# Attention scores of a head pair: one PSUM allocation of two banks in place of two allocations of one bank

## The chip, the cores and the metric

The kernel runs on one core of one Trainium2 chip. The metric is device time in microseconds (us) of one execution. The engines are PE (matrix products, with PEld for its weight loads), DVE (vector), ACT (scalar), POOL (GpSimd) and SP, which issues the DMAs.

## The reference

The reference chains one attention block and two feed-forward blocks over 4 batches of 576 positions, 8 heads of 64.

```python
scores = (1/8) * q @ k.T                       # per batch and head, 576 x 576, causal mask
a = exp(scores - max); a /= a.sum() + 1e-9
local = a @ v
qp = phi(q)                                    # elu + 1
mem_out = (qp @ M_prev) / (qp @ z_prev + 1e-6)
x = g * mem_out + (1 - g) * local              # g = sigmoid(beta), per head; heads side by side: 512 columns
x = ((x @ w1) * (x @ w2)) @ w3 @ w_out         # 512 -> 1024 -> 1024 -> 512
out = (sigmoid(x @ w_gate) * (x @ w_val)) @ w_o # 512 -> 1536 -> 512
```

## The kernel before

The 8 heads are taken as 4 pairs `p`; one head of a pair lies on partitions 0 to 63, the other on 64 to 127. The 576 rows of queries are padded to 580 and cut into 5 row blocks `i` of 116. Row block `i` has 116*(i+1) columns of scores. For `i = 4` these are 580, more than a PSUM bank holds, so they are made in two halves of 290 columns (`n` = 0, 1).

One step of attention runs as follows. `s_part` (L552) makes the scores of both heads (`hh` = 0, 1) in PSUM. One DVE instruction for each head (L557) adds the mask, writes the result to SBUF (`p`) and takes the row extremum into `sm`; this text calls it the mask. ACT takes the exponential (`e_part`, L105). `n_part` (L580, L581, L583) makes the reciprocal on DVE and normalises both heads on POOL or DVE; in the startup always on POOL. PE transposes the result (`t_part`, L613) and multiplies it with `v` into `o` (`a_part`, L666 to L681), to which the memory part (`qt`, `mphi`) is added.

Names in the rows: `s0_1_4_1_0` is the score of batch 0, pair 1, row block 4, half 1, head 0. `t0_1_3` are transposes of row block 3 of pair 1. The last number of a name is a running number.

Weights arrive as 64-bit floats. They are converted in steps: ACT makes `cy` and `cr` (L199, L202), DVE shifts and masks bits (L210, L211), POOL adds (L215), then a split into a high and a low half on ACT and on DVE or POOL (L311, L313) gives tiles `wslot` and `wo`. In the startup PE multiplies `w3` with `w_out` once: eight blocks `wps0_0` to `wps0_7` of twelve products (L302), each with the weights `wo0` to `wo3`, and then eight more (`wps1_`) with `wo4` to `wo7`, two of them ahead of the first feed-forward product and the rest between such products. The buffers of `wo4` to `wo7` are those of `wo0` to `wo3`, and so are free only when `wps0_7` has been made.

The order of work: in the startup, which holds attention of batch 0 and the blocks `wps0_0` to `wps0_7`, a scheduler that keeps a timeline of its own at build time sets the order on each engine. From there on the order on PE is the program's: attention of batch `b + 1` is laid in small steps between the feed-forward products of batch `b` (`drive`), and the scheduler orders the other engines.

PSUM has 8 banks. The pools take 3 (`ps_f`, for feed-forward sums and some transposes), 2 (`ps_s`, scores), 1 (`ps_t`, transposes) and 2 (`ps_o`). A tile's buffer is given again when all that read the tile are done.

Of the kernel before, what the change touches and what calls it, by code (L numbers as in the profile page):

```python
# [7 lines left out]
F32 = mybir.dt.float32  # L8
# [9 lines left out]
T = 116  # L18
# [32 lines left out]
def tile_attention_memory_ffn(  # L51
# [20 lines left out]
    fp = ctx.enter_context(tc.tile_pool(name="fp", bufs=2))  # L72
    ap = ctx.enter_context(tc.tile_pool(name="ap", bufs=2))
    ps_f = ctx.enter_context(tc.tile_pool(name="ps_f", bufs=3, space=bass.MemoryType.PSUM))
    ps_s = ctx.enter_context(tc.tile_pool(name="ps_s", bufs=2, space=bass.MemoryType.PSUM))
    ps_t = ctx.enter_context(tc.tile_pool(name="ps_t", bufs=1, space=bass.MemoryType.PSUM))
    ps_o = ctx.enter_context(tc.tile_pool(name="ps_o", bufs=1, space=bass.MemoryType.PSUM))
    dr = ctx.enter_context(tc.tile_pool(name="dr", bufs=1, space=bass.MemoryType.DRAM))
# [370 lines left out]
    def attention(b, lag):  # L449
# [79 lines left out]
        def s_part(p, i, n):  # L529
            w = T * (i + 1)  # L530
            if n == 0:
                ps_ = []
                for hh in range(2):
                    name = f"p{b}_{p}_{i}_{hh}"
                    if first and np_["n"] % 2 == 0:
                        m = np_["n"] // 2 % P0
                        ps_.append(fp.tile([T, 2 * S], F32, tag=f"h{m}", name=name, bufs=1)[:, :SP])
                    else:
                        ps_.append(ap.tile([T, SP], F32, tag="p", name=name, bufs=PB))
                    np_["n"] += 1  # L540
                sp[p, i] = (ps_, ap.tile([T, 8], F32, tag="sm", name=f"sm{b}_{p}_{i}", bufs=6))
            ps_, sm = sp[p, i]
            c0, c1 = (0, w) if w <= 512 else ((0, SP // 2), (SP // 2, SP))[n]
            os_ = []
            for hh in range(2):
                ps = ps_s.tile([128, 512], F32, tag="s", name=f"s{b}_{p}_{i}_{n}_{hh}")
                os_.append(ps[:T, : c1 - c0])
            terms = [(qks[p], qks[p])] if first else [(parts[p][x], parts[p][y]) for x, y in ((0, 0), (1, 0), (0, 1))]
            for x, (q_, k_) in enumerate(terms):
                for hh in range(2):  # L550
                    r = slice(64 * hh, 64 * hh + 64)
                    nc.tensor.matmul(  # L552
                        os_[hh], q_[r, 0, i * T : (i + 1) * T], k_[r, 1, c0:c1],
                        start=x == 0, stop=x == len(terms) - 1,
                    )
            for hh in range(2):
                nc.vector.tensor_tensor_reduce(  # L557
                    out=ps_[hh][:, c0:c1],
                    in0=os_[hh],
                    in1=msk[:, SP - w + c0 : SP - w + c1],  # L560
                    scale=-0.125,
                    scalar=3.0e38 if n == 0 else sm[:, 2 * hh : 2 * hh + 1],
                    op0=ALU.add,
                    op1=ALU.min,
                    accum_out=sm[:, 2 * hh + n : 2 * hh + n + 1],
                )
# [140 lines left out]
        for k in range(NPAIR * NT + lag):  # L707
# [3 lines left out]
            if k < NPAIR * NT:  # L711
                p, i = divmod(k, NT)
                wgt = 0.25 + 0.25 * (i + 1)
                s_part(p, i, 0)
                yield wgt
                if i == NT - 1:
                    s_part(p, i, 1)
                    yield 0.0
                if i == 0:
                    mem = mem_steps(p)  # L720
                next(mem, None)
                e_part(p, i, 0)
                yield wgt + between(kk % NT)
                e_part(p, i, 1)
                yield wgt + between(kk % NT)
                n_part(p, i)
                if i > 0:
                    next(mem, None)
                if i == 3:
                    qt_part(p)  # L730
                if i == 0:
                    load_qk(p + 2 if first else p + 1)
                if i == 4:
                    split_qk(p + 1)
                if i == 4:
                    load_rest(p + 1)
                yield wgt + between(kk % NT)
                yield wgt + between(kk % NT)
                yield wgt + between(kk % NT)
            while ts:  # L740
                yield ts.pop(0)()
            if kk >= 0 and kk % NT == NT - 1:
                p = kk // NT
# [143 lines left out]
```

## Time and profile before

| | |
|---|---|
| median of 3 runs | 1093.98 us (1088.79 to 1095.29) |
| profiled execution | 1093.54 us |
| its span, first to last instruction | 1091.6 us |
| PE busy | 1059.9 us, 97% |
| DVE, ACT, POOL busy | 506.6, 486.9, 319.7 us |

The profiled execution is 0.44 us below the median. 1.94 us of it lie outside the span. PE's busy time counts every stretch in which a product is under way; products overlap, so the same busy time can hold more or fewer of them.

### The profile page before, as it was taken

Reading aid. Unit: us, or ns where it says so; the run is one execution under the profiler, and the core shown is the slowest. Engines: PE = TensorE matmul, PEld = TensorE weight load, DVE = VectorE, ACT = ScalarE, POOL = GpSimd, SP = SyncE. Lnnn points to the kernel's source line nnn. Section 1 sums busy time; section 2 is a strip of 40 time slices with the busy share of each in tenths; the row PEclk is TensorE's granted clock in tenths of the full one; section 3 lists DMA queues with packets and bytes.
Section 4 is the critical chain, followed back from the end, with each engine's and each line's share of the span. In section 5 each row is a group of like instructions: output and inputs, shape, how many; then the busy total and the mean of one; then the engine's idle time right before and its main releaser. Section 6 shows DMA issues by size and latency. Waiting matters only on the chain.

```text
span 1091.6 us, 19687 instructions
## 1 busy us (share of the span) xinstructions
PE 1059.9 (97%) x7616; PEld 947.9 (87%) x7616; DVE 506.6 (46%) x1215; ACT 486.9 (45%) x1066; POOL 319.7 (29%) x260
## 2 busy tenths in 40 slices
PE   6999899999999899999999999999999999999998
PEld 3555677898998799889999899889999899999998
DVE  7996898758666605554222506453223402212210
ACT  6787676666766625444222415444223312222210
POOL 5887676446655602222000303231000200000000
PEclk9999899999999899999999999999999999999999
DMA  8565688856888564444445365433455355554451
GB/s 274 164 228 174 227 252 273 301 180 232 302 280 297 193 215 157 164 148 151 160 155 174 123 199 160 136 129 117 157 174 169 99 155 179 169 169 164 158 178 56
DMA packets 69237, 201.75 MB, mean 185 GB/s; under 512 B 9624, under 2 KB 15896, under 8 KB 69144
## 3 DMA queue, kind: packets, MB, share of 16 engines
q1 hardware_dynamic: 69144, 200.50, 56.0%
q8 instruction: 60, 0.98, 0.4%
q14 instruction: 33, 0.27, 0.1%
HBM read 160.10 MB, written 40.37 MB: 184 GB/s over the span
## 4 chain that ended last, share of the span: by engine, by line
PE 65%; DVE 1%; DMA 1%; ACT 1%; issue 0%; POOL 0%; ACTq 0%; POOLq 0%
PE gv L302 21%; PE ab L302 15%; PE ot L302 13%; PE xw L302 7%; PE s L552 3%; PE t L613 2%; PE o L681 2%; PE o L666 1%; DMA k<-wslot 1%; PE o L674 1%; DMA r<-in_o_dram 0%; PE qt L650 0%; DVE wraw L210 0%; DVE wslot L313 0%; DVE p L557 0%
## 5 line engine op out<-in xcount | busy, mean ns | idle before, releaser
L302 PE MATMUL gv<-x,wslot 128*128 128x288 f32 x2304 | 308.6, 295 | 4.5 <-ACT gsb L105 3.0
L302 PEld LDWEIGHTS gv<-x,wslot 128*128 128x128 f32 x2304 | 305.9, 188 | 6.8 <-ACT gsb L105 3.7
L302 PE MATMUL ab<-x,wslot 128*128 128x288 f32 x1536 | 227.8, 300 | 0.0
L302 PEld LDWEIGHTS ab<-x,wslot 128*128 128x128 f32 x1536 | 207.0, 188 | 11.2 <-issue 8.2
L302 PE MATMUL ot<-hg,wslot 128*128 128x288 f32 x1152 | 166.2, 301 | 3.7 <-DVE hg L313 3.6
L302 PEld LDWEIGHTS ot<-hg,wslot 128*128 128x128 f32 x1152 | 156.5, 190 | 10.1 <-issue 4.6
L583 POOL TENSOR_SCALAR p<-p,sm,omg 116x116 f32<-116x116 f32 (+4 forms) x100 | 97.7, 980 | 213.0 <-DVE sm L581 137.3
L215 POOL TENSOR_TENSOR wraw<-wraw,cr 128x512 int32<-128x512 int32 x76 | 109.9, 1458 | 66.5 <-DVE wraw L211 60.6
L105 ACT ACTIVATE p<-p,sm 116x116 f32<-116x116 f32 (+4 forms) x160 | 93.0, 582 | 63.7 <-DVE sm L557 55.9
L557 DVE CUSTOM_DVE_ANT_0 p<-s,msk 116x116 f32<-116x116 f32 (+4 forms) x160 | 68.5, 454 | 109.7 <-PE s L552 109.4
L417 DVE TENSOR_TENSOR hgraw<-gv,gsb 128x288 f32<-128x288 f32 x96 | 43.8, 457 | 157.4 <-PE gv L302 134.5
L302 PE MATMUL xw<-h,wslot 128*128 128x288 f32 x768 | 111.4, 299 | 0.0
L302 PEld LDWEIGHTS xw<-h,wslot 128*128 128x128 f32 x768 | 103.1, 188 | 3.6 <-issue 2.5
L105 ACT ACTIVATE gsb<-gv 128x288 f32<-128x288 f32 x96 | 39.4, 411 | 108.6 <-PE gv L302 108.6
L495 POOL TENSOR_TENSOR me<-mphi,z 116x640 f32<-116x640 f32 x16 | 25.4, 1586 | 175.2 <-issue 174.4
L613 PE MATMUL t<-idf,p 116*116 116x116 f32 x480 | 69.7, 274 | 3.7 <-POOL p L583 2.6
L199 ACT ACTIVATE cy<-r 128x512 f32<-128x512 f32 x76 | 50.6, 675 | 50.6 <-issue 27.9
L613 PEld LDWEIGHTS t<-idf,p 116*116 116x116 f32 x480 | 54.6, 140 | 18.8 <-POOL p L583 7.9
L211 DVE SCALAR_TENSOR_TENSOR wraw<-cy,wraw 128x512 int32<-128x512 int32 x76 | 66.6, 898 | 0.2
L373 DVE TENSOR_TENSOR hraw<-ab,asb 128x288 f32<-128x288 f32 x64 | 29.2, 456 | 67.7 <-PE ab L302 65.0
L313 POOL TENSOR_TENSOR wslot<-wraw,wslot 128x512 fp32r<-128x512 f32 x36 | 47.9, 1330 | 35.2 <-ACT wslot L311 35.0
L311 ACT CAST hg<-hgraw 128x576 fp32r<-128x576 f32 x48 | 32.4, 674 | 57.8 <-DVE hgraw L417 57.8
(78 smaller groups left out, 1129.4 us busy)
## 6 DMA issues: line engine op xcount, KB each, us to landing
wslot<-k SPq DMA_DIRECT2D x180, 512.0 KB, 3.5
k<-wslot SPq DMA_DIRECT2D x60, 512.0 KB, 5.2
r<-in_gv_dram SPq DMA_DIRECT2D x24, 512.0 KB, 5.3
qk<-in_qk_dram SPq DMA_DIRECT2D x32, 290.0 KB, 3.8
r<-in_w3t_dram SPq DMA_DIRECT2D x16, 512.0 KB, 4.0
r<-in_w_dram SPq DMA_DIRECT2D x16, 512.0 KB, 5.1
r<-in_o_dram SPq DMA_DIRECT2D x12, 512.0 KB, 5.6
qnr<-in_qn_dram SPq DMA_DIRECT2D x16, 320.0 KB, 3.2
```

Source lines behind the costliest of these rows:

```text
L105: ins = nc.scalar.activation(**kw)
L199: nc.scalar.mul(y, hi, 2.0**-112)
L211: nc.vector.scalar_tensor_tensor(z, y, -(2**31), z, ALU.bitwise_and, ALU.bitwise_or)
L215: nc.gpsimd.tensor_tensor(z, z, tmp["r"], ALU.add)
L302: nc.tensor.matmul(ps, w[:, wi, blk, :], x[:, xi, cols : cols + n], start=first and part == 0, stop=last and part == 2,)
L311: nc.scalar.copy(dst[:, 0], src)
L313: eng.tensor_sub(dst[:, 1], src, dst[:, 0].bitcast(F32))
L417: nc.vector.tensor_mul(hraw[:, c0 : c0 + HS], pss[1][:, :HS], asb)
L552: nc.tensor.matmul(os_[hh], q_[r, 0, i * T : (i + 1) * T], k_[r, 1, c0:c1], start=x == 0, stop=x == len(terms) - 1,)
L557: nc.vector.tensor_tensor_reduce(out=ps_[hh][:, c0:c1], in0=os_[hh], in1=msk[:, SP - w + c0 : SP - w + c1], scale=-0.125, scalar=3.0e38 if ...
L583: lower(SHARE_N).tensor_scalar(ps_[hh][:, :w], ps_[hh][:, :w], sm[:, 6 + hh : 7 + hh], omg[:T, 2 * p + hh : 2 * p + hh + 1], ALU.mult, ALU ...
L613: nc.tensor.transpose(tp[:T, c : c + T], src[hh][:, j * T : (j + 1) * T], idf[:T, :T])
```

## The change

The pool of the scores has one buffer of two banks. `s_part` allocates one tile for both heads, and head `hh` takes bank `hh` of it. The products, the masks and the PSUM taken are the same as before.

```diff
-    ps_s = ctx.enter_context(tc.tile_pool(name="ps_s", bufs=2, space=bass.MemoryType.PSUM))
+    ps_s = ctx.enter_context(tc.tile_pool(name="ps_s", bufs=1, space=bass.MemoryType.PSUM))
...
-            os_ = []
-            for hh in range(2):
-                ps = ps_s.tile([128, 512], F32, tag="s", name=f"s{b}_{p}_{i}_{n}_{hh}")
-                os_.append(ps[:T, : c1 - c0])
+            ps = ps_s.tile([128, 2, 512], F32, tag="s", name=f"s{b}_{p}_{i}_{n}")
+            os_ = [ps[:T, hh, : c1 - c0] for hh in range(2)]
```

In the built program the first score product of a tile now waits for both masks of the tile before it; it used to be one wait for each head, on that head's own mask. The mask of head 0 now waits for the products of both heads. A name such as `s0_1_4_1` now stands for both heads, and line numbers behind the change are smaller by 2.

The order on PE differs in the first 316 of its 7,280 products, up to the block `wps0_5`, and is the same from there. The orders on the other engines differ most in the same stretch.

On DVE, in the startup, between the masks of the two halves of row block 4 of pair 0. Before:

```order
L210 TENSOR_SCALAR wraw1_337<-cy2_319 128x512
L211 SCALAR_TENSOR_TENSOR wraw1_337<-cy2_319,wraw1_337 128x512
L557 ISA p0_0_4_0_293,sm0_0_4_295<-s0_0_4_1_0_305,msk_82,sm0_0_4_295 116x290
L557 ISA sm0_0_4_295 116x1
L210 TENSOR_SCALAR wraw1_337<-cy3_406 128x512
L313 TENSOR_TENSOR wo1_302<-wraw0_219,wo1_302 128x512
L557 ISA p0_0_4_1_294,sm0_0_4_295<-s0_0_4_1_1_306,msk_82,sm0_0_4_295 116x290
```

Now (the masks of the first half stand just ahead of this piece):

```order
L210 TENSOR_SCALAR wraw2_479<-cy4_473 128x512
L313 TENSOR_TENSOR wo2_374<-wraw1_331,wo2_374 128x512
L211 SCALAR_TENSOR_TENSOR wraw2_479<-cy4_473,wraw2_479 128x512
L210 TENSOR_SCALAR wraw2_479<-cy5_486 128x512
L313 TENSOR_TENSOR wo3_450<-wraw1_331,wo3_450 128x512
L211 SCALAR_TENSOR_TENSOR wraw2_479<-cy5_486,wraw2_479 128x512
L210 TENSOR_SCALAR wraw3_572<-cy6_551 128x512
L211 SCALAR_TENSOR_TENSOR wraw3_572<-cy6_551,wraw3_572 128x512
L210 TENSOR_SCALAR wraw3_572<-cy7_641 128x512
L211 SCALAR_TENSOR_TENSOR wraw3_572<-cy7_641,wraw3_572 128x512
L313 TENSOR_TENSOR wslot1_524<-wraw2_479,wslot1_524 128x512
L555 ISA p0_0_4_0_289,sm0_0_4_291<-s0_0_4_1_300,msk_82,sm0_0_4_291 116x290
```

The conversions of `cy4` to `cy7` moved ahead of the second half's masks. Counted up to the reciprocal of that row block (L581 on `sm0_0_4`), 14 more DVE instructions stand ahead than before: 5 of L210, 5 of L211, 4 of L313.

On PE, in the startup, around the block `wps0_1`. Before, from the second half of row block 4 of pair 1:

```order
L552 MATMUL s0_1_4_1_0_546<-qk0_1_172 116x290
L613 MATMUL t0_1_2_0_1_606<-idf_80,p0_1_2_1_413 116x116 x3
L552 MATMUL s0_1_4_1_1_547<-qk0_1_172 116x290
L302 MATMUL wps0_1_619<-wo0_247,wslot1_534 128x512 x3
L302 MATMUL wps0_1_619<-wo1_302,wslot1_534 128x512 x3
L302 MATMUL wps0_1_619<-wo2_382,wslot1_534 128x512 x3
L302 MATMUL wps0_1_619<-wo3_460,wslot1_534 128x512 x3
L552 MATMUL s0_2_0_0_0_590<-qk0_2_207 116x116
L552 MATMUL s0_2_0_0_1_591<-qk0_2_207 116x116
L613 MATMUL t0_1_3_0_0_639<-idf_80,p0_1_3_0_451 116x116 x4
```

Now, from the last products of the block:

```order
L302 MATMUL wps0_1_606<-wo3_450,wslot1_524 128x512 x3
L550 MATMUL s0_1_4_0_530<-qk0_1_172 116x290 x2
L672 MATMUL o0_1_726<-pq0_1_185,vs0_1_327 64x232 x2
L611 MATMUL t0_1_3_0_0_625<-idf_80,p0_1_3_0_442 116x116 x4
L611 MATMUL t0_1_3_0_1_631<-idf_80,p0_1_3_1_443 116x116 x4
L550 MATMUL s0_1_4_1_535<-qk0_1_172 116x290 x2
L550 MATMUL s0_2_0_0_578<-qk0_2_206 116x116 x2
L550 MATMUL s0_2_1_0_617<-qk0_2_206 116x232 x2
L611 MATMUL t0_1_4_0_0_665<-idf_80,p0_1_4_0_527 116x116
L611 MATMUL t0_1_4_1_681<-idf_80,p0_1_4_0_527 116x116
```

Both halves of row block 4 moved from ahead of `wps0_1` to behind it, and the heads stand side by side. Around `wps0_3` it is the same for the second half of pair 2.

On POOL, at the end of the startup, around the split of `wo7`. Before:

```order
L215 TENSOR_TENSOR wraw10_1439<-wraw10_1439,cr20_1416 128x512
L215 TENSOR_TENSOR wraw10_1439<-wraw10_1439,cr21_1467 128x512
L215 TENSOR_TENSOR wraw11_1535<-wraw11_1535,cr22_1524 128x512
L313 TENSOR_TENSOR wo7_1271<-wraw7_1205,wo7_1271 128x512
L215 TENSOR_TENSOR wraw11_1535<-wraw11_1535,cr23_1557 128x512
```

Now:

```order
L215 TENSOR_TENSOR wraw10_1412<-wraw10_1412,cr20_1389 128x512
L215 TENSOR_TENSOR wraw10_1412<-wraw10_1412,cr21_1440 128x512
L313 TENSOR_TENSOR wo7_1246<-wraw7_1181,wo7_1246 128x512
L215 TENSOR_TENSOR wraw11_1507<-wraw11_1507,cr22_1496 128x512
L215 TENSOR_TENSOR wraw11_1507<-wraw11_1507,cr23_1529 128x512
```

The split of `wo7` moved ahead of one conversion. On ACT the cast of `wo7` has one `cy` and one `cr` fewer ahead of it.

## Rows read from the trace of the kernel before

**Rows 1.** Stretches: length; busy us of PE, PEld, DVE, ACT, POOL; granted clock; DMA share, GB/s.

```profile
0.00:46.60 46.60, 36.53 (x99) 18.18 (x99) 37.28 (x95) 33.84 (x79) 32.03 (x31) 1.00 0.71 228
46.60:56.17 9.57, 9.30 (x51) 4.63 (x49) 9.08 (x18) 7.29 (x16) 8.39 (x8) 1.00 0.57 172
56.17:106.43 50.26, 47.72 (x266) 27.89 (x265) 41.70 (x109) 40.29 (x99) 41.04 (x39) 1.00 0.62 198
106.43:131.90 25.47, 22.24 (x104) 16.36 (x103) 22.10 (x40) 16.81 (x36) 16.85 (x13) 0.87 0.69 225
131.90:1091.60 959.70, 944.15 (x7103) 880.85 (x7102) 396.43 (x956) 388.64 (x838) 221.43 (x172) 1.00 0.55 181
```

**Rows 2.** The same view, score products alone (L552).

```profile
56.17:106.43 50.26, 14.95 (x55) 5.62 (x54) 1.00 0.62 198
```

**Rows 3.** Timeline of PE in the startup: start, us, count, [idle before].

```profile
41.89 4.71 PE L302 MATMUL wps<-wo,wslot 128*128 128x512 f32 x11
...
56.17 3.06 PE L302 MATMUL wps<-wo,wslot 128*128 128x512 f32 x12
59.16 0.46 PE L552 MATMUL s<-qk 64*116 64x116 f32 x4
...
62.29 0.65 PE L552 MATMUL s<-qk 64*116 64x232 f32 x4
...
65.40 0.85 PE L552 MATMUL s<-qk 64*116 64x348 f32 x4
...
67.41 1.03 PE L552 MATMUL s<-qk 64*116 64x464 f32 x2 [0.72 <-DVE sm L557]
...
76.68 0.75 PE L552 MATMUL s<-qk 64*116 64x290 f32 x4
...
78.70 0.74 PE L552 MATMUL s<-qk 64*116 64x290 f32 x2
...
127.16 4.96 PE L302 MATMUL wps<-wo,wslot 128*128 128x512 f32 x12
```

**Rows 4.** Groups on DVE in the first 46 us: busy us, mean ns.

```profile
L211 DVE SCALAR_TENSOR_TENSOR wraw<-cy,wraw 128x512 int32<-128x512 int32 x9 | 9.5, 1051 | 0.1
...
L210 DVE TENSOR_SCALAR wraw<-cy 128x512 int32<-128x512 int32 x9 | 5.4, 599 | 0.1
L313 DVE TENSOR_TENSOR wo<-wraw,wo 128x512 fp32r<-128x512 f32 x4 | 4.8, 1191 | 0.0
```

**Rows 5.** Timeline: DVE's first instruction; reciprocal and normalising of row block 4, pair 0.

```profile
5.48 0.17 DVE L777 TENSOR_SCALAR g<-g 128x8 f32<-128x8 f32 x1 [5.48 <-ACT g L776]
...
28.24 0.15 DVE L581 RECIPROCAL sm<-sm 116x2 f32<-116x2 f32 x1
...
28.57 2.84 POOL L583 TENSOR_SCALAR p<-p,sm,omg 116x580 f32<-116x580 f32 x2 [1.07 <-DVE sm L581]
```

**Rows 6.** Timeline: row block 4 of pair 1, from mask to transposes.

```profile
57.36 0.51 DVE L557 CUSTOM_DVE_ANT_0 p<-s,msk,sm 116x290 f32<-116x290 f32 x1
...
58.25 0.77 ACT L105 ACTIVATE p<-p,sm 116x580 f32<-116x580 f32 x1
...
62.38 2.62 POOL L583 TENSOR_SCALAR p<-p,sm,omg 116x580 f32<-116x580 f32 x2 [0.40 <-DVE sm L581]
...
63.30 0.71 PE L613 MATMUL t<-idf,p 116*116 116x116 f32 x5 [0.35 <-POOL p L583]
...
65.06 0.41 PE L613 MATMUL t<-idf,p 116*116 116x116 f32 x2 [1.04 <-POOL p L583]
```

**Rows 7.** Line L552 from 105 to 900 us: PE's idle time before it, by releaser.

```profile
  DVE sm L557: 4.9, 9
```

**Rows 8.** Timeline: the split of wo7 and the products behind it.

```profile
123.94 0.73 PE L302 MATMUL wps<-wo,wslot 128*128 128x512 f32 x2 [1.60 <-ACT wo L311]
...
124.51 1.73 POOL L313 TENSOR_TENSOR wo<-wraw,wo 128x512 fp32r<-128x512 f32 x1
...
126.30 0.80 PE L302 MATMUL wps<-wo,wslot 128*128 128x512 f32 x1 [1.62 <-POOL wo L313]
```

## The prediction

> **What bounds the kernel now.** I read the busy times by stretch first [rows 1]. From 131.90 us to the end PE has a product under way in 944.15 of 959.70 us, and the order on PE there is the same after the change. The startup, 0 to 131.90 us, is where orders move, so it is cut at places that both kernels have: the end of the weight block wps0_0 (46.60 us), the starts of wps0_1 (56.17) and wps0_5 (106.43), and the first feed-forward product (131.90). In the first stretch PE is busy 36.53 of 46.60 us, in the next two 9.30 of 9.57 and 47.72 of 50.26, and in the last 22.24 of 25.47. DVE is nearly as full: 37.28, 9.08, 41.70 and 22.10 us. So the startup has no single bound: PE, DVE and POOL are linked by the chain score, mask, exponential, reciprocal, normalising, transposes, and the weight conversion lies between on DVE, ACT and POOL.
>
> Next come the costs on PE. Two heads on the two halves of the partitions run side by side: four 290-column products of two heads take 0.75 us, two products of one head alone 0.74 us [rows 3]. A second head that stands alone costs as much as the pair. In the startup many heads stand alone before; now none does.
>
> PE's speed is the third thing to see. Eleven weight products take 4.71 us at 41.89, twelve take 3.06 us at 56.17 and 4.96 us at 127.16 [rows 3]. In the stretch from 106.43 the mean granted clock is 0.87, elsewhere 1.00 [rows 1]; the view also prints 1.00 for the first stretch, though the products there, 0.43 us each, are as slow as at the lower of the two levels (1.2 and 2.4 GHz), and those at 56.17 take 0.255.
>
> **The change part by part.** Products, masks and PSUM stay; waits and order change. I take the stretches in turn, against the profiled execution of 1093.54 us, whose span is 1091.6 (0.44 us under the median; I count it as equal).
>
> *To the end of wps0_0.* The transposes of row block 4 of pair 0 must come before wps0_0, and they need its reciprocal and normalising. The reciprocal ran at 28.24 us, and the normalising of both heads took 2.84 us [rows 5]. Now 14 more DVE instructions stand ahead of it: 5 x 0.599 + 5 x 1.051 + 4 x 1.191 = 13.0 us [rows 4] (for the two splits into wslot I take the time of those into wo). That would put it at 41.2 us, less what DVE's idle time takes up: DVE is idle 46.60 - 37.28 = 9.3 us here [rows 1], of which 5.48 lie ahead of its first instruction [rows 5], so at most 3.8 us. So it comes at 37.4 to 41.2, the normalising is done at 40.2 to 44.1, then the last five transposes take 0.71 [rows 6] to twice that at the lower speed, and the block 12 x 4.71 / 11 = 5.1 us: its end comes at 46.0 to 50.6 us, which is -0.6 to +4.0 against 46.60. I take +2, near the middle. What covered this before was slack: the normalising was done at 31.4 us, and eleven of the block's products only began at 41.89 [rows 3, 5].
>
> *wps0_0 to wps0_1.* The four lone scores of row block 4 of pair 1 leave this stretch (4 x 0.74), the 348-column pair of row block 2 enters (0.85 [rows 3]). That is -2.1 us, and the idle 0.27 us [rows 1] may go too. The first part of o0_1 moves in from the next stretch; it nets out over the two. Against it stands a wait for row block 2's normalising, which was well ahead before. I take -1, from -2.3 to +2.
>
> *wps0_1 to wps0_5.* Scores fill 14.95 us of PE here [rows 2]. In the new order the stretch holds the pairs of both halves for pair 1 (2 x 0.75) and two full sets, 0.46 + 0.65 + 0.85 + 1.03 + 2 x 0.75 = 4.49 each [rows 3] (for 464 columns a lone head's time, taken as the pair's). So 10.48 us, or -4.5. PE's idle time here is 50.26 - 47.72 = 2.5 us, which the new order may remove. The cost: the second half of row block 4 stood ahead of wps0_1 and wps0_3, whose 3 us hid the chain to its transposes. Now it stands behind them, with only the pairs 0.46, 0.65 and 0.85 and five transposes (0.71) between, 2.7 us of work. The chain as such is two masks of 0.51, two exponentials of 0.77, 0.3 for the reciprocal and 2.62 for the normalising [rows 6], 5.5 us; so PE waits 2.8 us each time. By what it took before, with the conversion between, it is longer: the mask ended at 57.87, the last transposes started at 65.06 [rows 6], 7.2 us, 8.2 with the masks, and the wait would be 5.5. Two pairs: 5.6 to 11 us. Where head 1's exponential runs beside head 0's normalising, it might be 4. Other row blocks wait for a mask more, 0 to 2 us. Sum: from -4.5 - 2.5 + 4 = -3 to -7 + 11 + 2 = +6. I take +1, nearer to the row than to the bare chain, because POOL and DVE stay over 80% busy here.
>
> *wps0_5 to the first feed-forward product.* The first score of batch 1 moves in here (+0.4), and the transposes of pair 3 follow their scores closely (0 to +2, taken +0.5). PE waited 1.60 and 1.62 us for wo7 [rows 8]. Its split on POOL started at 124.51, though the cast that it needs was done by 123.94; the conversion ahead of it is now behind. With one cy and one cr fewer ahead of the cast on ACT, I take -1.1 (0 to -2). The block behind it ran at the lower clock, 4.96 where 3.06 is the other level; whether the shorter wait keeps the clock is open: half of 1.9, -1. Sum -1.2, from -3.5 to +2.5.
>
> *After 131.90.* The order on PE is the same. In batches 1 to 3 the heads already alternate, and head 1's wait comes one product behind head 0's, so waiting for both masks at once moves only head 0's first product. From 105 to 900 us PE and PEld idle 4.9 us before scores because of masks, in 9 places [rows 7]. Twelve fifth row blocks could wait one mask longer, but head 1 waited for that mask anyway. +0.5, from -2 to +2. Fewer semaphore waits and signals: no row shows their price; they can give back some of those 4.9 us at most, and I take 0.
>
> Sum: +2 - 1 + 1 - 1.2 + 0.5 = +1.3. 1093.54 + 1.3 is 1094.9; I say **1095 us**.
>
> **The rivals.** *Startup stalls in full, slower.* Both exposures at their long end and wps0_0 late: +4 + 2 + 6 + 2 = +14, 1107 us. For it: POOL and DVE queues are full, and PE cannot pass a waiting transpose. Against: conversion has been done earlier by then, so the queues are freer. It decides over 1% when the two exposures come to about 7 us each (-7 + 14 + 1 there, +4 and -1 ahead of it). Chance 0.10.
>
> *PE drops to its lower level in the waits.* At 124 us PE worked 0.73 us between waits of 1.60 and 1.62, and the products after that were slow [rows 3, 8]; the new waits at pairs 1 and 2 look alike. Five blocks at 4.96 in place of 3.06 cost 9.5 us: with the +1.3, 1104 us, and a few us more with slow scores. Against: waits of 1.04 us in the same stretch left the clock at 1.00 [rows 1, 6]. Chance 0.05. The Trainium skill speaks for this one ("TensorE: Matmul & The Clock Gate", section on a second failure mode, PSUM-queue depth-cycling): when a kernel cycles PSUM buffers so that PE pauses often between groups of products, the clock swings between its levels. This trace shows one such swing in the startup, at 0.87.
>
> *The work freed on PE is kept, faster.* If the chain to the transposes hides whole behind other work, the stretches give -0.6, -2.3, -4.5 - 2.5 and -3.5, together -13.4: 1080 us. For it: 6.6 us of scores on PE are gone for certain, and the conversion is further on. Against: 2.7 us of work would have to hide a chain of 5.5. It decides over 1% when both exposures together stay under 2.5 us. Chance 0.09.
>
> *It does nothing.* The moved orders cancel and the pairing saves time that PE would have waited anyway: 1093.5 us. PE's later stretch sets the time, and it is equal. Chance 0.16; it cannot be told from my forecast by time, only by the stretches.
>
> **How the numbers follow.** The forecast has 0.60. A measurement here tells about 1%, 11 us, from no change. Faster by more than that: the third rival, 0.09. Slower: the first two, 0.15. Within: 0.76. The range of 8 in 10 goes over the forecast and no effect, with the unknown terms combined (about -6 and +7 around 1095) and the spread of the runs, some 3 us: 1086 to 1105 us.
>
> **What would show it.** wps0_0 ends at 47 to 50 us; all scores of the startup show as pairs (x4 in a row for each tile); lone-score time on PE in the startup falls by 6 us or more; PE waits on POOL ahead of transposes grow from 1.4 us to over 5 in the two places behind wps0_1 and wps0_3; the wait at wo7 falls under 3 us; wps0_5 starts within 5 us of 106.43; the stretch from the first feed-forward product to the end keeps its 959.7 us within 2. I am wrong if that last stretch changes by more, if the order at 46 us costs over 5 us, or if the clock falls inside 46 to 106 us.

## The result, and the profile after

The changed kernel takes 1110.31 us (median, 1109.67 to 1110.45) where the kernel before takes 1093.9 in the same comparison: a ratio of 1.0147, interval 1.0127 to 1.0167. It is slower by 16 us, outside the range of the prediction. The profiled execution took 1110.45 us, with a span of 1108.6.

First come the busy times of the changed kernel by stretch, cut at the same places as [rows 1]: the end of `wps0_0`, the starts of `wps0_1` and `wps0_5`, the first feed-forward product.

```profile
0.00:50.20 50.20, 25.21 (x93) 13.72 (x93) 41.98 (x88) 35.17 (x80) 35.48 (x31) 0.80 0.73 239
50.20:65.29 15.09, 10.38 (x59) 5.66 (x58) 13.73 (x28) 10.21 (x23) 14.67 (x14) 0.82 0.58 181
65.29:122.54 57.25, 48.63 (x261) 29.36 (x259) 31.62 (x102) 34.40 (x87) 30.15 (x33) 0.87 0.43 134
122.54:145.96 23.42, 20.75 (x111) 14.89 (x110) 18.30 (x36) 16.88 (x38) 14.56 (x11) 1.00 0.56 196
145.96:1108.60 962.64, 943.71 (x7103) 880.86 (x7101) 406.05 (x963) 389.35 (x842) 224.66 (x174) 0.99 0.55 182
```

Against [rows 1] the five stretches changed by +3.6, +5.5, +7.0, -2.1 and +2.9 us, together +17.0, the difference of the spans. PE did less: its busy time to the first feed-forward product is 104.97 us where it was 115.79. Its idle time there is 40.99 us where it was 16.11. So the loss is waiting, ahead of 146 us above all. The clocks of the first stretch, 0.80 here and 1.00 before, are no difference of speed at its end: twelve products of `wps0_0` take 5.00 us here, eleven took 4.71 there [rows 3].

The scores alone, by the same stretches; the third answers to [rows 2]:

```profile
0.00:50.20 50.20, 9.22 (x34) 3.58 (x34) 0.80 0.73 239
50.20:65.29 15.09, 1.87 (x8) 0.54 (x8) 0.82 0.58 181
65.29:122.54 57.25, 11.34 (x56) 4.23 (x56) 0.87 0.43 134
122.54:145.96 23.42, 1.10 (x12) 0.77 (x12) 1.00 0.56 196
```

That is 23.5 us of scores in the startup; the same view of the kernel before sums to 39.6. Pairing did what it says. PE's other products take 81.4 us to the first feed-forward product, 76.2 before.

PE's timeline of the changed kernel, with the instructions that ended long waits (in brackets: idle time ahead, and who ended it); it answers to [rows 3, 6]:

```profile
27.85 0.75 PE L550 MATMUL s<-qk 64*116 64x290 f32 x4
...
37.07 0.74 PE L550 MATMUL s<-qk 64*116 64x116 f32 x4 [6.72 <-DVE sm L555]
41.23 1.12 PE L550 MATMUL s<-qk 64*116 64x232 f32 x4 [3.42 <-DVE sm L555]
...
58.48 0.71 PE L638 MATMUL qt<-idf,mphi 116*128 116x116 f32 x5 [1.49 <-POOL mphi L504]
62.09 2.18 PE L664 MATMUL o<-qts,ms 64*64 64x232 f32 x8 [2.89 <-ACT qts L644]
...
75.47 0.71 PE L611 MATMUL t<-idf,p 116*116 116x116 f32 x5 [0.92 <-POOL p L581]
...
99.38 1.51 PE L611 MATMUL t<-idf,p 116*116 116x116 f32 x10 [1.48 <-POOL p L581]
...
115.11 0.64 PE L611 MATMUL t<-idf,p 116*116 116x116 f32 x2 [3.32 <-POOL p L581]
...
142.67 0.50 PE L302 MATMUL wps<-wo,wslot 128*128 128x512 f32 x1 [2.17 <-POOL wo L313]
...
169.06 0.59 PE L550 MATMUL s<-qkh 64*116 64x290 f32 x2 [3.37 <-DVE sm L555]
```

Behind the wait for the first load, the two longest end at 37 and 41 us, at the first scores of pair 1. The two places that the prediction priced at 5.6 to 11 us, ahead of the transposes of row block 4 behind `wps0_1` and `wps0_3` (75.47 and 99.38), cost 0.92 and 1.48.

What the first score of pair 1 waits for is seen on DVE's timeline of the changed kernel, which answers to [rows 4, 5]. The masks are the two at 36.06 and 36.50; the scores that they read are those at 27.85 on PE, done at 28.60.

```profile
28.16 0.68 DVE L211 SCALAR_TENSOR_TENSOR wraw<-cy,wraw 128x512 int32<-128x512 int32 x1
28.76 0.79 DVE L210 TENSOR_SCALAR wraw<-cy 128x512 int32<-128x512 int32 x1
29.58 1.63 DVE L211 SCALAR_TENSOR_TENSOR wraw<-cy,wraw 128x512 int32<-128x512 int32 x1
32.47 1.40 DVE L210 TENSOR_SCALAR wraw<-cy 128x512 int32<-128x512 int32 x1 [1.25 <-ACT cy L199]
33.90 1.64 DVE L211 SCALAR_TENSOR_TENSOR wraw<-cy,wraw 128x512 int32<-128x512 int32 x1
35.46 0.68 DVE L313 TENSOR_TENSOR wslot<-wraw,wslot 128x512 fp32r<-128x512 f32 x1
36.06 0.51 DVE L555 CUSTOM_DVE_ANT_0 p<-s,msk,sm 116x290 f32<-116x290 f32 x1
36.50 0.08 DVE L555 DVE_READ_ACCUMULATOR2_ANT sm<- 116x1 f32 x1
36.50 0.51 DVE L555 CUSTOM_DVE_ANT_0 p<-s,msk,sm 116x290 f32<-116x290 f32 x1
```

From 28.60 to 36.06 us DVE works on conversions, one of which itself waits 1.25 us for ACT, while finished scores lie in PSUM; PE stands still from 30.35 us on. And the conversions done early bring little. The instructions of L199 (one makes a `cy`, the start of each conversion) by stretch, in the kernel before (new rows) and in the changed one:

```profile
28.00:46.60 18.60, 3.33 (x5) 1.00 0.58 169
46.60:65.00 18.40, 3.32 (x5) 1.00 0.66 214
65.00:86.00 21.00, 2.73 (x4) 1.00 0.67 214
```

```profile
28.00:46.60 18.60, 3.29 (x5) 0.53 0.64 199
46.60:65.00 18.40, 4.04 (x6) 0.78 0.62 186
65.00:86.00 21.00, 0.00 (x0) 0.88 0.42 136
```

To 65 us the changed kernel has started 18 conversions (7 of them ahead of 28 us) where the kernel before has 16; then none for 21 us. The conversion has run ahead and then stops, and the later ones come late: the twenty-third starts at 137.8 us where it started at 118.8. In the program a conversion needs one of three `wraw` buffers; that this is what stops it was not tested. DVE is then busy 22.67 of the 24 us from 146 us (20.96 of the 24 us from 132 in the kernel before), and masks of batch 1 come late there (169.06). That the late conversions are the reason is a reading of the trace.

### The profile page after: what moved, and what is told of

Its sections match the earlier page's. It is cut to its first block, busy times and chain, and to the rows that moved or that the text cites. A ratio compares the mean times of both kernels' runs of the same rounds, so it can differ in the third digit from the quotient of the medians.

```text
span 1108.6 us, 19687 instructions
## 1 busy us (share of the span) xinstructions
PE 1048.7 (95%) x7616; PEld 944.5 (85%) x7616; DVE 511.7 (46%) x1215; ACT 486.0 (44%) x1066; POOL 319.5 (29%) x260
## 4 chain that ended last, share of the span: by engine, by line
PE 65%; DVE 1%; DMA 1%; ACT 1%; issue 0%; DVEq 0%; ACTq 0%
PE gv L302 21%; PE ab L302 14%; PE ot L302 14%; PE xw L302 7%; PE s L550 3%; PE t L611 2%; PE o L679 2%; PE o L664 1%; PE o L672 1%; DMA r<-in_o_dram 1%; PE qt L648 0%; DVE wraw L210 0%; DVE p L555 0%; DVE wraw L211 0%; DVE wslot L313 0%
## 5 line engine op out<-in xcount | busy, mean ns | idle before, releaser
L581 POOL TENSOR_SCALAR p<-p,sm,omg 116x116 f32<-116x116 f32 (+4 forms) x100 | 96.7, 970 | 228.1 <-DVE sm L579 151.9
L215 POOL TENSOR_TENSOR wraw<-wraw,cr 128x512 int32<-128x512 int32 x76 | 110.9, 1473 | 72.2 <-DVE wraw L211 64.2
L199 ACT ACTIVATE cy<-r 128x512 f32<-128x512 f32 x76 | 50.3, 673 | 53.7 <-issue 31.7
L211 DVE SCALAR_TENSOR_TENSOR wraw<-cy,wraw 128x512 int32<-128x512 int32 x76 | 61.1, 829 | 0.3
L302 PE MATMUL wps<-wo,wslot 128*128 128x512 f32 x192 | 55.9, 439 | 2.2 <-POOL wo L313 2.2
```

The costliest lines, as they stand in the source:

```text
L199: nc.scalar.mul(y, hi, 2.0**-112)
L211: nc.vector.scalar_tensor_tensor(z, y, -(2**31), z, ALU.bitwise_and, ALU.bitwise_or)
L215: nc.gpsimd.tensor_tensor(z, z, tmp["r"], ALU.add)
L302: nc.tensor.matmul(ps, w[:, wi, blk, :], x[:, xi, cols : cols + n], start=first and part == 0, stop=last and part == 2,)
L581: lower(SHARE_N).tensor_scalar(ps_[hh][:, :w], ps_[hh][:, :w], sm[:, 6 + hh : 7 + hh], omg[:T, 2 * p + hh : 2 * p + hh + 1], ALU.mult, ALU ...
```

## The experiments

Three theories were set up. A: the order that the scheduler chose for the startup is the loss. B: the longer wait (a score product waits for both masks of the tile before) is the loss, in any order. C: a part of it is made in batches 1 to 3. Later came a fourth, D: two tiles that PE and DVE worked on in turn became one. A ratio below is to the kernel before, measured beside each.

**Which batches.** The score pool is opened anew behind batch 0, and only one side takes the tile of two banks.

```diff
+            if s_pool.get("first") != first:
+                s_pool["first"] = first
+                score_pool(first)        # later_both: score_pool(not first)
...
+        s_pool["ctx"] = tc.tile_pool(name=f"ps_s{both}", bufs=1 if both else 2, space=bass.MemoryType.PSUM)
```

> Batch 0 takes one tile of two banks for both heads, batches 1 to 3 two tiles of one bank as before. Theory A (the loss is made in the startup, by the order that the scheduler chose there): 1108 to 1111 us, all of the +17. Theory B (the loss is made in the startup, by the longer wait itself): the same. Theory C (a part is made in batches 1 to 3, where the last stretch grew by 2.9 us): 1106 to 1108, 3 us less than the changed kernel.

Measured: 1115.04 us, 1.0191 (1.0159 to 1.0223). PE's order is that of the changed kernel, and the other engines' nearly so. This is above all three ranges. The 4.7 us over the changed kernel lie behind the startup: its first feed-forward product starts at 145.80 us (145.96 in the changed kernel), and from there to the first one of batch 1 it takes 286.30 us (281.35).

> The other half: batch 0 as before, one tile for both heads in batches 1 to 3 alone. Theories A and B: 1093 to 1095 us, no change. Theory C: 1096 to 1098, the 2.9 us of the last stretch.

Measured: 1095.58 us, 1.0009 (0.9985 to 1.0033). All of the loss comes with batch 0. In batches 1 to 3 no effect shows; the interval leaves room for at most 3.6 us, and the time lies between the two ranges. In the profiled execution the stretch from the first feed-forward product to that of batch 1 takes 275.23 us, not more than the 278.41 of the kernel before, which speaks against theory C.

This execution shows something else. Its PE order is that of the kernel before, and it starts `wps0_1` 0.6 us later than that kernel but `wps0_3` 3.0 us later. Between them the granted clock is low for about 7 us while PE hardly waits:

```profile
65.50:72.40 6.90, 6.74 (x17) 3.46 (x18) 6.85 (x15) 5.99 (x17) 6.20 (x7) 0.55 0.59 186
```

So in this stretch, where PE is nearly always busy, the low clock is lost time.

**Order against wait.** All instructions of each engine are held to a given order by dependencies that set the order alone and make nothing wait. The order is taken from the other kernel's built program.

```diff
+    for e, ranks in ORDER.items():
+        mine = [i for i in nc.cur_bb.bb.instructions if i.engine == getattr(mybir.EngineType, e) ...]
+        row = [mine[r] for r in ranks] + mine[len(ranks) :]
+        for x, y in zip(row, row[1:]):
+            tc.add_manual_dep(y, x.name, mybir.DependencyInfo(mybir.DependencyClass.NoSync, ...), reason="order")
```

> The kernel before with its two tiles of one bank and its waits for each head's own mask, but on every engine in the order of the changed kernel. Theory A (order): 1107 to 1111 us, as the changed kernel. Theory B (wait): 1093 to 1097, near the kernel before, since no product waits for the other head's mask. If both count, between them: then the distance to 1110.3 is what the waits cost in the new order.

Measured: 1114.12 us, 1.0180 (1.0149 to 1.0211). With the waits of the kernel before, the new order costs as much as the change; the intervals overlap, 3 us above theory A's range. (What the added dependencies cost by themselves was not measured alone; in one_fill below, held in the same way to the changed kernel's own order, `wps0_0` starts at 45.53 us where it was 45.25.) PE's waits by what ended them, to 124 us of this kernel and to 122.5 us of the changed one (`s` on `sm` and `t` on `p`, each: us in total, times, longest):

```profile
PE s L552 <- DVE sm L557: 12.6, 5, 6.4
PE t L613 <- POOL p L583: 12.5, 9, 3.3
```

```profile
PE s L550 <- DVE sm L555: 14.1, 8, 6.7
PE t L611 <- POOL p L581: 12.2, 9, 3.3
```

The same waits stand there without the longer one. In this order it adds 1.5 us of waiting ahead of scores, and the time isn't longer for it.

> The changed kernel with its one tile of two banks and its longer waits, but on every engine in the order of the kernel before. Theory A (order): 1093 to 1097 us. Theory B (wait): 1105 to 1111. The lone heads of the old order stay; a product of head 0 then also waits for the mask of head 1 that stands between.

Measured: 1144.86 us, 1.0462 (1.0424 to 1.0499), more than either theory had for it. PE's waits to 190 us:

```profile
PE s L550 <- DVE sm L555: 34.6, 18, 3.3
```

In the old order the heads stand apart, with conversions between their masks, and 18 times a score waits for masks; in the kernel before it was 8 times, 7.3 us. Not all of the 51 us is waiting: to the first feed-forward product PE idles 30.4 us more than before, and its busy time is 23.4 us longer, at mean granted clocks of 0.80 and 0.73 between 59.54 and 159.70 us. So theory B is right for the old order and A for the new. One may read it so: the scheduler's order avoids some 35 of the 51 us that the longer wait would cost, and the 16 that stay are the price of avoiding them.

**Parts of the order.** First the conversions at 28 to 42 us: on DVE, ACT and POOL the masks, exponentials and normalising were moved ahead of `cy6` and `cy7`; the rest of the order is the changed kernel's. (The edit is written here as moves; the kernel holds each engine's order as a list of numbers.)

```diff
+move("DVE", ["ISA p0_0_4_0 (half 1)", "ISA p0_0_4_1 (half 1)"], before="L210 cy6")
+move("DVE", ["ISA p0_1_0_0", "ISA p0_1_0_1", "L578 sm0_0_4", "L579 sm0_0_4"], before="L210 cy7")
+move("DVE", ["ISA p0_1_1_0", "ISA p0_1_1_1"], before="L313 wslot1")
+move("ACT", ["L105 p0_0_4_0", "L105 p0_0_4_1"], before="L311 wslot0"), and of p0_1_0 before="L311 wslot1"
+move("POOL", ["L581 p0_0_4_0", "L581 p0_0_4_1"], before="L313 wslot0")
```

> The changed kernel in its own order but for the first 46 us: on DVE the masks of row block 4's second half of pair 0, its reciprocal and the masks of row blocks 0 and 1 of pair 1 stand ahead of the conversions of cy6 and cy7, on ACT the exponentials and on POOL the normalising go with them. PE's order is untouched. If the conversions ahead of these masks are what makes PE wait 6.72 and 3.42 us there: both waits fall under 2 us, wps0_0 ends 5 to 9 us sooner, and the time falls by 2 to 8 us (POOL, full from 42 us on, gives the rest back). If the waits only move on behind: 1109 to 1112 with wps0_1 where it was.

Measured: 1111.84 us, 1.0152 (1.0124 to 1.0179), no gain. PE's timeline of this kernel:

```profile
33.33 0.65 PE L550 MATMUL s<-qk 64*116 64x232 f32 x4 [2.59 <-DVE sm L555]
...
36.76 5.11 PE L302 MATMUL wps<-wo,wslot 128*128 128x512 f32 x12
...
45.76 0.79 PE L679 MATMUL o<-pt,vs 116*64 116x344 f32 x2 [3.11 <-ACT pt L629]
50.45 0.45 PE L611 MATMUL t<-idf,p 116*116 116x116 f32 x1 [3.90 <-POOL p L581]
...
62.70 2.18 PE L664 MATMUL o<-qts,ms 64*64 64x232 f32 x8 [2.89 <-ACT qts L644]
```

`wps0_0` now runs at 36.76 us in place of 45.25, so the conversions ahead of the masks were the wait there. But the 8.5 us are given back by 62.70, where PE waits as it did at 62.09. POOL's normalising of `p0_1_0` and the memory part of pair 1 still stand behind conversions there. Moving one place only moves the wait on.

> Two tiles with their own waits as before; PE is held to the changed kernel's order (scores in pairs, row block 4 behind the weight blocks), and the scheduler orders the other engines anew for it. If the order on PE is the loss: 1107 to 1114 us. If it is the order on DVE, ACT and POOL that came with the longer wait: 1092 to 1102.

Edit: the block of dependencies above for PE alone. Measured: 1113.58 us, 1.0169 (1.0146 to 1.0192), the first case; but what the scheduler made for the other engines is a new order as well, so this alone doesn't put the loss on PE's.

> The changed kernel's tile of two banks and its waits; DVE, ACT, POOL and SP are held to the order of the kernel before, and the scheduler orders PE anew (scores in pairs). If the loss is the conversions that moved ahead of the masks: 1090 to 1100 us. If the longer wait cannot live with DVE's old order, where masks of the two heads stand apart with conversions between: 1110 to 1145.

Edit: the same block for DVE, ACT, POOL and SP, on the changed kernel. Measured: 1112.47 us, 1.0161 (1.0136 to 1.0187), the second case, at its lower end. Here `wps0_1` starts 0.4 us sooner than before (55.81), and most of the loss lies behind `wps0_4`: +5.0 us at its start, +14.9 at that of `wps0_5`. DVE's and then PE's timeline of this kernel there:

```profile
100.03 0.52 DVE L555 CUSTOM_DVE_ANT_0 p<-s,msk 116x348 f32<-116x348 f32 x1 [2.58 <-PE s L550]
...
105.40 0.64 DVE L555 CUSTOM_DVE_ANT_0 p<-s,msk 116x464 f32<-116x464 f32 x1 [3.66 <-PE s L550]
...
108.91 0.75 PE L550 MATMUL s<-qk 64*116 64x290 f32 x4 [3.56 <-DVE sm L555]
...
114.33 1.32 PE L550 MATMUL s<-qk 64*116 64x290 f32 x4 [1.65 <-DVE sm L555]
```

DVE waits for PE's scores and PE for DVE's masks by turns. So going back to the old order on the other engines doesn't win the loss back while the longer wait stands. Whether PE's order alone would cost as much with two tiles is left open, since no run combines it with the old order of the others.

**The clock.** Idle products were put in front of five of PE's waits, to keep it at work there.

```diff
+        FILL = {("t", 1, 4, 0): 1, ("t", 2, 4, 1): 2, ("t", 3, 2, 0): 3, ("qt", 1): 1, ("a", 1): 3}
+                x = nc.tensor.matmul(dst[:T, :512], idf[:T, :T], msk[:, :512], start=True, stop=True)
```

> The changed kernel in its own order, with ten idle products more (116x512, the identity by the mask, overwritten afterwards) just ahead of five places where PE waited: one at the first transposes into qt0_1, three at the first product of o0_1, one at the transposes t0_1_4_0, two at t0_2_4_1, three at t0_3_2_0. No result uses them. Theory K (the clock's fall to its lower level behind those waits is a loss of its own): the low spells between 57 and 121 us go and the time falls by 3 to 8 us, to 1102 to 1107. Theory W (what is waited for on POOL, DVE and ACT sets the pace, whatever PE's clock): 1108 to 1112, the time that PE gains it waits elsewhere.

Measured: 1111.22 us, 1.0148 (1.0120 to 1.0176), inside the range of theory W. But the trace doesn't bear theory W out. In the changed kernel the granted clock is at the lower level for 20.5 us between 57 and 122 us, in four spells; with the fill 10.2 us are left, in two. Rows of this kernel: the three idle products ahead of `o0_1`, the stretch from `wps0_1` to `wps0_5`, and the part of it from `wps0_2` on:

```profile
62.35 5.47 PE L534 MATMUL o<-msk,idf 116*116 116x512 f32 x6 [2.84 <-DVE x L314]
```

```profile
69.81:123.53 53.72, 48.73 (x273) 28.13 (x272) 31.77 (x102) 34.50 (x87) 29.32 (x31) 0.97 0.44 141
82.81:123.53 40.72, 37.39 (x217) 21.67 (x216) 25.55 (x78) 25.99 (x65) 25.01 (x27) 1.00 0.42 134
```

The three idle products (six records) did not fill a wait. Their buffer came free only at 62.35 us, about where the real products ran before (62.09), so they stand behind the wait and take 5.47 us of their own. `wps0_1` therefore starts 4.5 us later than in the changed kernel. From there to `wps0_5` it takes 53.72 us in place of 57.25, at a mean clock of 0.97 in place of 0.87, idle products included: 3.5 us are won. (That the other engines had 4.5 us more to run ahead may share in it.) The last stretch, at a mean clock of 0.93, gives back 1.6, and the first feed-forward product starts at 148.52 us (145.96). So the total says nothing on the clock. The stretch where the fill worked speaks for theory K, at the lower end of its 3 to 8 us. A fill without the three misplaced products wasn't tried.

**Depth of the buffers.** Theory D was tried by giving batch 0 other shares of PSUM. Only four banks hold two pairs, so `ps_f` had to shrink to one bank until the first feed-forward product, in a base as well.

```diff
-    ps_f ... bufs=3, ps_s ... bufs=1
+    ps_f.open("ps_f0", 1)      # 2 in f2_s3
+    ps_s.open("ps_s0", 2)      # tiles of one bank; f1_pair1: 1, f1_pair2: 2 tiles of two banks; f2_s3: 3 of one
```

> A base for the next two: batch 0 as in the kernel before, with two score tiles of one bank, but with one bank in place of three for the weight blocks and transposes (ps_f) until the first feed-forward product; from there as before. Fewer banks there cost something of their own, by estimate 0 to 25 us over the kernel before.

> The base with one tile of two banks for both heads in batch 0, one buffer (two banks left unused). Theory D (the loss is that two tiles which PE and DVE worked on in turn became one: PE waits while DVE masks and DVE waits while PE multiplies): 10 to 25 us over the base f1_s2. Rival (what is lost is an accident of the order that the scheduler happened to choose): within 5 us of the base, either way.

> The base with two such tiles of two banks, so four banks for scores. The heads still stand in pairs. Theory D: the loss against the base goes, within 4 us of f1_s2 or below it. Rival (scores in pairs are what harms, since a second head made at once cannot fill a later wait): as slow as f1_pair1.

> Batch 0 with three score tiles of one bank and two banks for ps_f. Theory D in the other direction: if depth of the score buffers sets the startup, a third gains, 1080 to 1092 us; if two are enough, the bank that ps_f lost decides, 1094 to 1105.

Measured: base 1141.29 us (1.0417, 1.0370 to 1.0464), one pair 1129.25 (1.0327, 1.0272 to 1.0382), two pairs 1129.69 (1.0328, 1.0283 to 1.0372), three single tiles 1107.64 (1.0113, 1.0072 to 1.0153). A second pair of buffers gains nothing, and the one tile is faster than two single ones by 12 us, which neither theory D nor its rival had. As the one tile lost nothing here, there was no loss for the second pair to win back, so f1_pair2 tests neither. The three single tiles lie above both ranges. All this is against theory D; but with one bank for `ps_f` the base takes 47 us more, 38.7 of them in its startup, so this doesn't settle it for the kernel at hand.

**Is it the tile or this order?** Both kernels got the same small shifts: the lag of the transposes behind the scores in the startup, and the share of the normalising on POOL.

```diff
-LAG0 = 3
+LAG0 = 2        # and 4
...
-SHARE_N = (1.0, 0.5, 0.5)
+SHARE_N = (0.8, 0.5, 0.5)
```

> The kernel before with the transposes of the startup written two row blocks behind their scores in place of three (LAG0 = 2): the scheduler gets the same work with another start and another order. If the time before was one favourable order among many (theory L): 1098 to 1115 us. If any order that the scheduler makes with two score tiles keeps close to it (theory D, depth): 1088 to 1100.

> The changed kernel with LAG0 = 2. Theory D: 10 to 25 us over before_lag2, since the one tile is still one. Theory L: anywhere from 1095 to 1125, its distance to before_lag2 no longer +17, perhaps of the other sign.

> The kernel before with LAG0 = 4. Theory L: 1098 to 1115 us. Theory D: 1088 to 1100.

> The changed kernel with LAG0 = 4. Theory D: 10 to 25 us over before_lag4. Theory L: a distance that differs from +17 by 8 us or more.

> The kernel before with one in five of the startup's normalisings on DVE in place of POOL (SHARE_N 0.8). POOL, over 80% busy from 46 to 106 us, gets relief, by the rows 1.3 to 1.9 us for each normalising moved, 8 of 40. If POOL's load sets the startup: 1084 to 1092 us, better than both kernels. If the order decides: 1095 to 1112.

> The changed kernel with the same share. If the loss belongs to the one tile: 10 to 25 us over before_norm8. If it belongs to the order: a distance between -8 and +8 us. If POOL's load sets the changed kernel's startup: below 1103.

Measured, with two landmarks of each profiled execution: the start of the first feed-forward product (the startup), and from there to the first one of batch 1.

| | two tiles, us | one tile, us | distance of medians | startup, two / one | first product to batch 1's, two / one |
|---|---|---|---|---|---|
| as given (`LAG0` 3) | 1093.9 | 1110.31 | +16.4 | 131.95 / 145.96 | 278.41 / 281.35 |
| `LAG0` 2 | 1107.80 | 1105.50 | -2.3 | 135.62 / 140.79 | 287.57 / 281.59 |
| `LAG0` 4 | 1100.23 | 1107.97 | +7.7 | 129.11 / 137.28 | 285.21 / 287.37 |
| `SHARE_N` 0.8 | 1101.93 | 1114.37 | +12.4 | 131.47 / 143.15 | 287.74 / 288.20 |

Behind batch 1's first product every one of these takes 681.2 to 681.6 us. By the ranges, the pairs with `LAG0` 2 and 4 speak for the order and the pair with `SHARE_N` 0.8 for the tile. The two landmarks part the two. The startup is longer with the one tile each time, by 14.0, 5.2, 8.2 and 11.7 us. The startups with two tiles are 129.1 to 135.6 us, those with one tile 137.3 to 146.0. They don't overlap, their means differ by 9.8 us, and later_both (134.96) and startup_both (145.80), which run the two given orders again, lie inside. The stretch behind it varies by up to 10 us with the order, but not with the tile: the four means are 284.7 and 284.6. There the kernel before as given has the shortest of the eight. Each shift makes the kernel before slower, by 6 to 14 us (ratios 1.0127, 1.0057 and 1.0056, whose intervals all begin at 1.0037 or above).

So both hold in part: with three banks for `ps_f` the tile costs the startup some 10 us in the orders that the scheduler makes for it, and its total of +16 also contains that the kernel before stood on the best order of those tried. Each landmark comes from one execution. No kernel of the 18 is faster than the kernel before.

## Why the prediction failed, step by step

The step that failed is the price of the waits between `wps0_0` and `wps0_5`. The **sum by stretches** let PE's idle time there (0.27 and 2.5 us) go, or replaced it by two exposures; it rose to 4.71 and 8.62 us. To the end of `wps0_0` the sum was right: +2, measured +3.6, inside its bounds, and by its own mechanism. The reciprocal of row block 4 of pair 0 came at 41.29 us, just above the 37.4 to 41.2 that were said, and moving the masks ahead of the conversions takes 8.5 us off the block's start (one_masks).

**`wps0_0` to `wps0_1`** failed first: -1 was said, from -2.3 to +2, and +5.5 came. The scores did leave (3.93 to 1.87 us). But the prediction looked for a wait for row block 2's normalising, and what came was the memory part of pair 1: 1.49 us for `mphi` on POOL, 2.89 for `qts` on ACT. Both stand behind conversions:

```profile
55.40 1.81 POOL L313 TENSOR_TENSOR wslot<-wraw,wslot 128x512 fp32r<-128x512 f32 x1
57.18 1.25 POOL L504 TENSOR_TENSOR mphi<-mphi,mn 116x640 f32<-116x640 f32 x1
...
57.35 2.76 DVE L210 TENSOR_SCALAR wraw<-cy 128x512 int32<-128x512 int32 x2
...
60.80 0.67 ACT L199 ACTIVATE cy<-r 128x512 f32<-128x512 f32 x1 [2.88 <-DVE wraw L211]
61.38 0.68 ACT L644 COPY qts<-qt 128x348 f32<-128x348 f32 x2
```

The transposes that `qts` copies end at 59.19 us, but the copy stands on ACT behind the start of a conversion, which waits 2.88 us for one on DVE. POOL is busy 14.67 of 15.09 us in this stretch. The further conversions had been counted as far as the reciprocal of row block 4 of pair 0, and no further. What they displace on POOL and ACT behind it had no term.

**`wps0_1` to `wps0_5`**: +1 was said, +6 at most, and +7.0 came: 6.1 us of idle time and 0.9 of busy time. The two exposures that made up most of the risk were over-priced: 0.92 and 1.48 us, or 2.6 and 2.5 with the waits of the scores just ahead of them. With the 3.32 us at 115.11 they are 8.4 of the 8.62 us that PE idles. That third wait, ahead of transposes of pair 3, had no term. Its normalising stands on POOL behind conversions, though its reciprocal is done at 112.15:

```profile
111.55 2.89 POOL L215 TENSOR_TENSOR wraw<-wraw,cr 128x512 int32<-128x512 int32 x2 [1.36 <-DVE sm L578]
112.00 0.15 DVE L579 RECIPROCAL sm<-sm 116x2 f32<-116x2 f32 x1
...
114.43 1.24 POOL L581 TENSOR_SCALAR p<-p,sm,omg 116x348 f32<-116x348 f32 x2
```

The scores fell by 3.6 us (4.5 was said), and yet PE's busy time rose, at a mean clock of 0.87; one_fill, at 0.97, takes 3.5 us less. The sum had no term for a lower clock here.

**`wps0_5` to the first feed-forward product**: -1.2 was said, -2.1 came; the wait for `wo7` fell from 3.2 to 2.17 us [rows 8], and the clock stayed at 1.00, which the prediction had counted at half. **After it**: +0.5 was said, -2 to +2, and +2.9 came. The order on PE is the same, but DVE still had conversions to catch up; by the table above such a difference in this stretch comes with any order, so its cause stays open.

One argument of the prediction stands behind these steps: that conversion done earlier leaves the queues freer later. As a mean it was right. From `wps0_1` to `wps0_5` POOL is busy 30.15 of 57.25 us where it was 41.04 of 50.26, and DVE 31.62 where it was 41.70. But a queue that is free in the mean still held conversions at the places that PE waited for, and the work moved forward had displaced attention where that was urgent.

Of the **rivals**, the first had the sign and nearly the time (1107), but not its point: it decides when the two exposures come to 7 us each, and they came to 2.5. The second, the lower clock, did happen, in four spells, and it had a chance of 0.05. The Trainium skill ("TensorE: Matmul & The Clock Gate", section on a second failure mode, PSUM-queue depth-cycling) tells of a kernel in which PE often pauses between groups of products, the clock swings and throughput suffers. The trace agrees in the swings, with means of 0.82 and 0.87 in two stretches, though PE's pauses here are waits for masks, normalising and the memory part. The price was 9.5 us; what the runs show is up to 3.5 us, in the one stretch where one_fill held the clock. The third rival's premise was right and under-priced: scores on PE fell by 16.1 us in the startup, not 6.6, since the first stretch, with 20.07 us of scores before and 9.22 after, was left out of the count. None of it was kept.

Of the signs, pairs in place of lone scores showed, the fall of score time by over 6 us, and `wo7`'s wait; `wps0_0` ended at 50.2, a little behind 47 to 50. The waits ahead of the transposes at the two places, `wps0_5` within 5 us, and the last stretch within 2 did not. Two of the three signs of being wrong came: the last stretch changed by 2.9 us, and the clock fell between 46 and 106 us.

What stays open: how much of the +16 another order would save with the one tile. In the four pairs the startup's part was 5 to 14 us; a good order for the one tile, made by hand beyond the piece in one_masks, wasn't tried.

## What to carry to other kernels

Where a scheduler sets the order at build time, an edit of two lines is a new order for the whole startup; cost it by what each in-order queue holds ahead of the urgent chain, up to the end of the stretch and not to the first landmark. Work that is moved forward isn't won if it stands ahead of an urgent chain and then stops. Before filling waits to hold the clock, look in the trace whether the fill runs in the wait or behind it. And before a difference of 1% is put down to an edit, give both versions the same small shift of the order: here the distance went from +16 to -2 us.

## What the runs showed of the hardware

Between 57 and 122 us the clock fell to the lower level in four spells of the changed kernel, each with waits of PE ahead of it. One example: PE waited 3.32 us up to 115.11, and the mean granted clock was 0.52 from 114.18 to 121.01. With waits filled (one_fill) the clock held at 1.00 from 82.81 to 123.53 us, and the stretch from `wps0_1` to `wps0_5` was 3.5 us shorter. A spell of 6.9 us at 0.55 in later_both, with PE busy 6.74 of it, cost 2.4 us of delay between two blocks of PE.

DVE's bit operation L211 on 128x512, 0.68 us at 28.16, took 1.63 at 29.58 and 1.64 at 33.90. The two long ones ran beside POOL's additions L215 (29.24 to 32.35, 33.53 to 34.98), the short one beside POOL's normalising (25.42 to 29.27). No run tests whether that is the reason.
